# Two of the seven products of each second product taken in seven products of quarters, with attention in a new order between them

## The chip, the cores and the metric

The kernel runs on one core of one Trainium2 chip. Times are device microseconds of that core, from the first to the last instruction and a little around it; the profile's span is some 2 us shorter than the measured time (752.6 of 754.33 us in the profiled run before). A kernel is run several times, interleaved with runs of the kernel before on the same chip (e1 to e4 on one chip, e5 to e12 on another). A kernel counts as faster or slower only from 2% on.

Five engines work side by side: TensorE (PE in the profile; PEld is its weight load), VectorE (DVE), ScalarE (ACT), GpSimd (POOL) and SyncE (SP), in whose queue the transfers that the profile's page lists are issued. In a stretch of 81.61 us of the kernel before, TensorE was busy for 81.61 us, VectorE for 43.77 and ScalarE for 25.99. PSUM is the memory that the matmuls of this code write to; the code uses it in banks, and in the traces TensorE waits until a bank that it writes again has been read out: 0.32 us for one in block 1 of the changed kernel, up to 4.7 us in e10.

## The reference, cut to what matters

```python
# attention: B, H, S, Ns, D = 8, 8, 512, 32, 64, per batch b and head
xread = softmax(x @ state.T / 8) @ state        # 512 rows
sread = softmax(state @ x.T / 8) @ x            #  32 rows
x = concat(xread, sread) -> (8 * 544, 512)
# then two matrix products with an activation between
h = x @ w_in                                    # (4352, 512) @ (512, 2048)
g = h / (1 + exp(-1.702 * h))
out = g @ w_out                                 # (4352, 2048) @ (2048, 512)
```

All of it in float32. The second product, `g @ w_out`, of the 512 rows of a batch is what the change is about.

## The kernel before

A batch is a *block*. The 512 rows of block b go through the first product in an up phase (function `up_strassen`) and through the second in `strassen`. Both use seven products where a two by two split would need eight (the scheme of Strassen and Winograd). `strassen` splits `g` (512 x 2048, held transposed) into four quarters A11 to A22 and `w_out` (2048 x 512) into B11 to B22; S1, S2, S4 are sums of the A, T1 to T4 sums of the B, and S3 stands where A21 was. One of its seven products is this loop, of 16 matmuls with 256 columns (nb = 2, HF = 8, HN = 256):

```python
        def product(ps, lhs, rhs, first):
            for r in range(nb):
                for f in range(HF):
                    nc.tensor.matmul(
                        ps[:, r], lhs[f][:, P * r : P * (r + 1)], rhs[:, f],
                        start=(first and r == 0 and f == 0), stop=(f == HF - 1), skip_group_check=True,
                    )
                if todo:
                    for fn, args in todo.pop(0):
                        fn(*args)
```

After each half of a product comes one *slot*: a list of calls that work on the attention of block b + 1 (and, in the first slot, on the rest of block b's up phase). So attention is spread over the second product of the block in front:

```python
        at(0, att_state, b)
        for j in range(NPR):            # four
            at(j, att_xT, b, j)
        at(5, att_scores, b)
        at(5, att_M, b, 0)
        at(5, att_M, b, 1, True)
        ...                             # the softmaxes
        at(8, att_M, b, 2)
        at(8, att_M, b, 3, True)
        ...
        at(11, att_sread, b)
```

`att_state` and `att_xT` transpose on TensorE into a PSUM pool of two buffers and copy out on ScalarE:

```python
    psA = ctx.enter_context(tc.tile_pool(name="psA", bufs=2, space=bass.MemoryType.PSUM))

    def att_state(b):
        ps = att_ps([P, P], f"stT_{b}")                 # a buffer of psA
        nc.tensor.transpose(ps, stn[b].rearrange("p g d -> p (g d)"), ident)
        A[b]["stT"] = apool.tile([P, P], FP32, tag="stT", name=f"stT_{b}", bufs=2)
        nc.scalar.copy(A[b]["stT"], ps)
```

The end of the up phase, run in the first slot, puts two activations on ScalarE, each behind an addition on VectorE:

```python
        def end(u):
            ...
            add(product(u, "y", l22, t4, False), c21, c21)     # TensorE, then VectorE
            gelu(c21, c21)                                      # ScalarE
            add(product(u, "z", m4, b22, False), c12, c12)
            gelu(c12, c12)
```

Block 0's second product is taken without the scheme, and the 256 rows of `sread` of all batches come last, as a smaller stage (`_sr`).

## Time and profile before

| | before |
|---|---|
| time, median (range) | 754.42 us (754.26 to 754.55), 3 runs |
| span of the profiled run | 752.6 us |
| TensorE busy | 738.5 us, 98% |
| VectorE, ScalarE busy | 432.5 us (57%), 233.1 us (31%) |
| period of blocks 2 to 6 | 81.61 us |
| granted TensorE clock | 0.999 |

The period is the distance of the same instruction in two neighbouring blocks. It is the sharpest number here: it repeats to 0.01 us from block to block.

### The profile page before, as it was taken

What the parts mean: (1) busy time and instruction counts of PE and PEld (TensorE: products, weight loads), DVE (VectorE), ACT (ScalarE), POOL (GpSimd) and SP (SyncE); (2) the same over time, 40 slices, a digit from 0 to 9 for tenths busy, and PEclk for the clock granted to TensorE, in tenths of its full rate; (3) what the DMA queues carried; (4) which work ended last, traced back from release to release, by engine and by line L of the source; (5) the groups of instructions that cost most, each with busy time, mean ns of one, the idle gap of its engine ahead of it and who ended that gap; (6) DMA issues with size and microseconds to landing.
All of it is one profiled execution on the core that took longest, in us unless ns stands there. A gap on an engine that the chain in (4) does not pass through costs nothing.

```text
span 752.6 us, 10076 instructions
## 1 busy us (share of the span) xinstructions
PE 738.5 (98%) x4265; PEld 564.6 (75%) x4267; DVE 432.5 (57%) x744; ACT 233.1 (31%) x415; POOL 0.8 (0%) x8
## 2 busy tenths in 40 slices
PE   8989999999999999999999999999999999999997
PEld 3433444467888878887788788887888778888996
DVE  5999799642646383645637264638355563762341
ACT  4676511022324241433134232424143313300210
POOL 0000000000000000000000000000000000000000
PEclk9999999999999999999999999999999999999999
DMA  9811245010030000300030003000030000000000
GB/s 234 332 57 56 93 160 144 0 57 1 28 86 4 1 15 31 72 1 15 29 74 0 1 29 84 6 1 15 29 74 1 15 29 15 0 15 29 15 1 28
DMA packets 48764, 35.24 MB, mean 47 GB/s; under 512 B 36432, under 2 KB 44112, under 8 KB 48720
## 3 DMA queue, kind: packets, MB, share of 16 engines
q1 hardware_dynamic: 48720, 34.61, 16.0%
q8 instruction: 33, 0.54, 0.3%
q14 instruction: 11, 0.09, 0.0%
HBM read 25.69 MB, written 8.91 MB: 46 GB/s over the span
## 4 chain that ended last, share of the span: by engine, by line
PE 96%; SPq 2%; ACT 1%; DMA 1%; issue 0%; DVE 0%; ACTq 0%
PE y L483 19%; PE z L483 13%; PE x L483 13%; PE upy L614 8%; PE h L418 8%; PE o L436 7%; PE upz L614 6%; PE upx L614 6%; PE M L272 4%; PE xT L254 2%; PE upy_sr L614 1%; PE y_sr L483 1%; SPq L131 1%; PE sr L367 1%; PE s L272 1%; PE upz_sr L614 1%
## 5 line engine op out<-in xcount | busy, mean ns | idle before, releaser
L483 PE MATMUL x<-w_out,g 128*128 128x256 f32 x448 | 100.2, 379 | 0.0
L483 PEld LDWEIGHTS x<-w_out,g 128*128 128x128 f32 x448 | 84.3, 190 | 11.2 <-ACT osb L443 0.2
L624 DVE TENSOR_TENSOR g<-upy,g 128x512 f32<-128x512 f32 x72 | 48.1, 689 | 68.4 <-PE upy L614 68.4
L621 ACT ACTIVATE g<-g 128x512 f32<-128x512 f32 (+1 forms) x84 | 49.8, 600 | 100.5 <-DVE g L624 100.5
L347 ACT COPY M<-M 128x512 f32<-128x512 f32 x64 | 33.2, 596 | 95.1 <-PE M L272 95.1
L418 PE MATMUL h<-aT,M 128*128 128x512 f32 x128 | 58.2, 600 | 4.4 <-ACT M L347 4.4
L418 PEld LDWEIGHTS h<-aT,M 128*128 128x128 f32 x128 | 23.6, 190 | 36.7 <-issue 24.4
L483 PE MATMUL z<-sums,later 128*128 128x256 f32 x224 | 51.1, 382 | 0.0
L483 PE MATMUL z<-w_out,g 128*128 128x256 f32 x224 | 50.8, 382 | 0.0
L483 PE MATMUL y<-sums,later 128*128 128x256 f32 x224 | 50.5, 379 | 0.0
L483 PE MATMUL y<-sums,g 128*128 128x256 f32 x224 | 50.5, 379 | 0.0
L483 PE MATMUL y<-w_out,g 128*128 128x256 f32 x224 | 50.1, 382 | 0.0
L483 PEld LDWEIGHTS z<-sums,later 128*128 128x128 f32 x224 | 42.1, 190 | 10.4 <-issue 5.0
L483 PEld LDWEIGHTS y<-w_out,g 128*128 128x128 f32 x224 | 42.1, 190 | 10.4 <-issue 5.0
L614 PE MATMUL upx<-aT,M 128*128 128x256 f32 x192 | 49.3, 379 | 0.0
L614 PE MATMUL upy<-ta,M 128*128 128x256 f32 x192 | 49.3, 379 | 0.0
L483 PEld LDWEIGHTS z<-w_out,g 128*128 128x128 f32 x224 | 41.7, 190 | 6.1
L483 PEld LDWEIGHTS y<-sums,g 128*128 128x128 f32 x224 | 41.7, 191 | 5.1
L483 PEld LDWEIGHTS y<-sums,later 128*128 128x128 f32 x224 | 41.7, 191 | 5.1
L500 DVE TENSOR_TENSOR osb<-z,later 128x512 f32<-128x512 f32 x14 | 9.7, 692 | 58.4 <-PE z L483 58.4
L614 PEld LDWEIGHTS upy<-ta,M 128*128 128x128 f32 x192 | 36.5, 190 | 4.9
L614 PEld LDWEIGHTS upx<-aT,M 128*128 128x128 f32 x192 | 36.5, 190 | 4.9
(147 smaller groups left out, 1028.0 us busy)
## 6 DMA issues: line engine op xcount, KB each, us to landing
later<-in_moe_w_out_dram SPq DMA_DIRECT2D x16, 512.0 KB
out_dram<-osb SPq DMA_DIRECT2D x32, 256.0 KB
xn<-in_x_dram SPq DMA_DIRECT2D x28, 256.0 KB
w_out<-in_moe_w_in_dram SPq DMA_DIRECT2D x12, 512.0 KB
later<-in_moe_w_in_dram SPq DMA_DIRECT2D x4, 512.0 KB
sums<-in_x_dram SPq DMA_DIRECT2D x4, 256.0 KB
stn<-in_state_dram SPq DMA_DIRECT2D x16, 32.0 KB
out_dram<-osb_sr SPq DMA_DIRECT2D x4, 128.0 KB
```

The source lines that it names most:

```text
L131: nc.sync.dma_start(xn[b][:, c], x_v[b, c])
L254: nc.tensor.transpose(ps[:, c], x_heads(b, c, j), ident)
L272: nc.tensor.matmul(ps[g][st], A[b]["stT"][rows, st], rhs(rows, j), start=True, stop=True)
L347: nc.scalar.copy(m[:, g], ps[g])
L367: nc.tensor.matmul(ps[st, g], a["eT"][:, g, c, st], xn[b][:, c, NG * j + g], start=(c == 0), stop=(c == SCH - 1),)
L418: nc.tensor.matmul(hps, lhs[i], rhs[i], start=(i == 0), stop=(i == n - 1))
L436: nc.tensor.matmul(ops, G[key, f // 2][:, f % 2, P * r : P * (r + 1)], w_out[:, f], start=(f == 0), stop=(f == NF - 1))
L483: nc.tensor.matmul(ps[:, r], lhs[f][:, P * r : P * (r + 1)], rhs[:, f], start=(first and r == 0 and f == 0), stop=(f == HF - 1), skip_grou ...
L500: nc.vector.tensor_tensor(out=o, in0=ps, in1=with_, op=ALU.add)
L614: nc.tensor.matmul(ps[:, k], lhs[i][:, o : o + P], rhs[i], start=(first and k == 0 and i == 0), stop=(i == n - 1), skip_group_check=True,)
L621: nc.scalar.activation(out=dst, in_=src, func=AF.Gelu_apprx_sigmoid)
L624: nc.vector.tensor_tensor(out=dst, in0=ps, in1=x, op=ALU.add)
```

## The change

The intent: in blocks 2 to 7, two of the seven products, S2 T2 and S3 T3, are themselves taken by the scheme of seven, on quarters of their operands. A product of 16 matmuls with 256 columns becomes 28 matmuls with 128 columns, half the width, so 14 instead of 16 by columns. The price is additions on VectorE. Results are no longer accumulated in PSUM over two products but added by VectorE, some buffers are halved in number to make room, and attention is put into other slots. The core of the diff, with cuts:

```diff
-    opool = ctx.enter_context(tc.tile_pool(name="opool", bufs=2))
+    opool = ctx.enter_context(tc.tile_pool(name="opool", bufs=1))
...
+    def strassen_low(left, right, bank, R, at):
+        b11, t3, b21, b22, t1, t2, t4 = right
+        a11, a12, a21, a22, s1, s2, s4 = left
+        p, u2, u3 = (pu[:, i] for i in range(3))
+        o = [v[:, :P] for v in bank]
+        def product(ps, lhs, rhs):
+            for f in range(QF):                      # four
+                nc.tensor.matmul(ps, lhs[f], rhs[:, f], start=(f == 0), stop=(f == QF - 1))
+        ...
+        product(o[0], a11, b11)
+        nc.scalar.copy(p, o[0])
+        at(1)                                        # a hook: a piece of attention on VectorE
+        product(o[1], s2, t2)
+        add(u2, o[1], p)
+        at(2)
+        product(o[2], a12, b21)
+        add(c11, o[2], p)
+        at(3)
+        product(o[0], a21, t3)
+        add(u3, o[0], u2)
+        at(4)
+        product(o[1], s1, t1)
+        add(c22, o[1], u3)
+        add(c12, o[1], u2)
+        at(5)
+        product(o[2], a22, t4)
+        add(c21, o[2], u3)
+        at(6)
+        product(o[0], s4, b22)
+        add(c12, o[0], c12)
...
+    def strassen_two(key, dst, hooks):               # order of its products, with the names of their hooks
+        # P1 = A11 B11, P2 = A12 B21, P5 = S1 T1, P6 = S2 T2 (low), P4 = A22 T4, P7 = S3 T3 (low), P3 = S4 B22
...
+    def hooks_next(b):
+        at("P1a", att_state, b)
+        at("P1a", att_xT, b, 0)
+        at("P1a", att_xT, b, 1)
+        at("P1b", att_xT, b, 2)
+        at("P1b", att_xT, b, 3)
+        at("P2a", att_scores, b)
+        at("P2a", att_M, b, 0)
+        at("P2a", att_M, b, 1, True)
...
+        at("P4a", att_sread, b)
+        at("P4a", att_M, b, 3, True)
+        at("P4a", att_M, b, 2)
...
+        hooks["P1a"] = [(rest, ())] + hooks.get("P1a", [])   # rest: end of the up phase
```

"P1a" is the slot after the first half of P1, and so on. I call the two products taken in quarters the *low* products.

## The prediction

> **What bounds the kernel now.** I read the page first (busy time of each engine), then stretches of one attention block each, then the groups by shape, then the timeline in the order of the code.
>
> ```profile
> span 752.6 us, 10076 instructions
> PE 738.5 (98%) x4265; PEld 564.6 (75%) x4267; DVE 432.5 (57%) x744; ACT 233.1 (31%) x415; POOL 0.8 (0%) x8
> ```
>
> TensorE leads. Blocks 2 to 6 are alike: the chain that ended last finds the same first product at 240.06, 321.67, 403.28, 484.89 and 566.50, one period of 81.61. The stretch of block 3:
>
> ```profile
> 321.67:403.28 81.61, 81.61 (x507) 68.45 (x507) 43.77 (x72) 25.99 (x46) 0.00 (x0) 1.00 0.12 27
> ```
>
> PE fills all of it, VectorE 54% and ScalarE 32%. So a TensorE microsecond removed counts in full, and so does every wait that the change puts in front of TensorE; VectorE has 37.8 us of room.
>
> The price of a matmul comes from start-to-start distances, since 379 ns in the groups is one record's duration and records overlap. Rows of the timeline, N=256 and N=128 (the `_sr` stage at the end already runs float32 matmuls with 128 columns and one weight load each):
>
> ```profile
> 389.30 1.03 PE L614 MATMUL upx<-aT,M 128*128 128x256 f32 x4
> 390.17 1.03 PE L614 MATMUL upy<-ta,M 128*128 128x256 f32 x4
> ...
> 702.49 1.06 PE L614 MATMUL upx_sr<-srT,w_in 128*128 128x128 f32 x8
> 703.38 1.06 PE L614 MATMUL upy_sr<-ta_sr,ws 128*128 128x128 f32 x8
> ```
>
> A program matmul in float32 leaves two records: the loop over two groups of two blocks with 8 pieces is 16 matmuls, and the chain shows x32 for it, 6.91 us. Hence N=256 costs 0.863/2 = 0.432 us a matmul and N=128 0.893/4 = 0.223 us: half the columns cost 52%, although weight loads double per column.
>
> [...] The trace has 112 ns a record[...]. I use the 112.
> [...] (below: the copy of `stT` starts after two gelus although its transpose was long done). This carries my main loss.
> [...] The trace has 0.69 us for 512 and 0.42 for 256[...].
>
> **The change, part by part.**
>
> *Products.* In blocks 2 to 7, two of seven products (16 matmuls, N=256, 6.91 us) become seven of four matmuls, N=128: 28 x 0.2234 = 6.25 us. Saving 0.65 each, 12 of them: **-7.8 us**. That is the whole possible gain, 1.0%. The saving is small because 28 halves are 14 whole ones, and the 112 against 108 ns takes back a third of the two saved.
>
> *VectorE work.* Rows used:
>
> ```profile
> L461 DVE TENSOR_TENSOR later<-later,g 128x512 f32<-128x512 f32 x28 | 19.4, 692 | 1.0
> L537 DVE TENSOR_TENSOR ta<-aT 128x256 f32<-128x256 f32 x12 | 5.0, 417 | 0.0
> ```
>
> A 128x128 add is extrapolated to 0.29 us. Per block the change adds 2x7 such adds (4.1), four 512-wide left sums (2.8), eight 256-wide ones (3.4), two whole additions (k2+k1, k3+k2: 1.4) and, net, one result addition that ScalarE copied before (0.7), while the two removed k2/k3 adds (1.4) are about balanced by t01 and the halved softmax steps (0.7+0.7). Sum 12.4: 43.8 becomes 56 of 81 us, 69%. Not a bound on average. In order of the code, with P2's start at 0: score transposes 4.7 to 6.0, maxima to 7.5, the halved softmax to 10.2, the first result, S4 and the last left sum to 13.0, state normalisation to 14.6. The first low product starts at 16.6. Inside it each step of PE is 4 x 0.223 = 0.89 us, and VectorE has one add (0.29) plus a hook (0.66), 0.95; three PSUM banks rotate, so a bank is wanted again only two steps (1.8 us) after its product ended. Worked through step by step, bank 1 is read at 18.9 and wanted at 20.1, bank 0 20.8 against 21.9. No wait. The sums for the second low product end at 27.5, its start is 33.5; VectorE is clear at 32.6. I find no PE wait there, with about 1 us of margin.
>
> *Attention order.* The first slot (after half of P1) now holds the transposes of the state, of xT 0 **and** of xT 1. They share a PSUM pool of two buffers, so xT 1 waits for ScalarE's copy of `stT`. Before, xT 1 came 3.5 us later. Same place in block 3:
>
> ```profile
> 326.47 0.14 PEld L245 LDWEIGHTS stT<-ident,stn 128*128 128x128 f32 x1
> ...
> 326.75 0.63 ACT L621 ACTIVATE g<-g 128x512 f32<-128x512 f32 x1 [2.96 <-DVE g L624]
> 326.79 0.60 PE L254 MATMUL xT<-ident,xn 128*128 128x128 f32 x4
> ...
> 327.23 3.62 PE L483 MATMUL x<-w_out,g 128*128 128x256 f32 x16
> ...
> 327.61 0.63 ACT L621 ACTIVATE g<-g 128x512 f32<-128x512 f32 x1 [0.23 <-DVE g L624]
> 328.15 0.25 ACT L247 COPY stT<-stT 128x128 f32<-128x128 f32 x1
> ```
>
> The two gelus of the last up products come first in ScalarE's queue, and each waits for a VectorE add. The copy ends at 328.40; TensorE would be ready at 327.23. With 0.1 us to the weight load and 0.2 more to the first matmul, it resumes at 328.7: a wait of about 1.45 us. Blocks 2 to 6 have it (block 7 has no attention after it): **+7.2 us**, which eats the gain.
>
> The pieces of `sr`, M3 and M2 now stand in one slot. A change between full-array and small-tile matmuls costs some 0.1 us on each side (the 16 records after an M run take 3.56 instead of 3.45) and 0.16 within the M run. One such visit less in six blocks, partly kept between two tile shapes: estimate 0.2 each, **-1.2 us**. M2's second bank waits for the `sr` copy, which ends 0.5 us after, while M3 takes 0.86: hidden.
>
> *Buffers.* One `osb` buffer instead of two. At the end of block 0 ScalarE's four copies now each wait for a store (the third copy started at 158.69, 2.2 us after the first ended): the last ends near 164.8 instead of 160.1, the gelu behind it 4.6 us later, S2 near 167.0; the product that wants it starts at 167.8. Hidden. In the last stage results come 3.45 us apart and a store takes some 3: at most **+0.2 us** at the tail. The 6 extra sums in block 1 (4.1 us) fall into VectorE's idle time (6 and 7.7 us waits before its products).
>
> Sum: 754.4 - 7.8 + 7.2 - 1.2 + 0.2 = 752.8.
>
> **Rivals.**
> *The full gain*: the wait at xT 1 isn't there (or is mostly covered), giving 754.4 - 7.8 - 1.2 = 745.5. For it: the author moved these on purpose. Against: pool of two, program order[...]. I give it 12%.
> *VectorE sets the pace in the low products*: 0.95 against 0.89 us a step and a serial queue; if it enters late by 3 us, each low product waits 2 to 3 us, 12 x 2 = +24 us, 777. Against: it is clear 1 to 2 us before both, by measured durations. A slip in part, 0.3 us each, gives +4 (757). I give the large one 5%.
> *Weight loads bound at 128 columns*: the load rows read 190 ns each; unhidden that would be 56 x 0.19 = 10.6 us a product, +45 in all. The `_sr` stage refutes it: same loads, 112 ns apart. The left operand there is contiguous as here; I give it 2%.
>
> **Range and chances.** All small terms pull within 1%: the lower end is the full gain with little left over, the upper end the wait plus 0.4 us per low product. Being 2% faster (below 739.3) would need twice the saving that the matmuls can give: 0.01. 2% slower (above 769.5) needs 17 us of new waits beyond the one found: 0.06.
>
> **What would show it.** (1) The products of quarters: records of N=128 0.112 us apart, 6.25 us per low product; if 0.19, the third rival. (2) TensorE idle about 1.4 us at xT's second set in five blocks, released by ScalarE's `stT` copy; if absent, the first rival. (3) Idle of TensorE at the low products released by VectorE: should be under 0.3 us each; more means the second. (4) VectorE near 56 us a block. (5) Periods of blocks 2 to 6 near 81.4 us, block 7 1.3 shorter than before. The prediction fails if a wait that I did not find, most likely on a bank or through VectorE's queue, recurs in each block.

What the trace has: 112 ns a record, the order on ScalarE in which the copy of `stT` starts at 328.15, after the gelus of 326.75 and 327.61, and 0.69 and 0.42 us for an addition of 512 and 256 columns. The sum reads 754.4 - 7.8 + 7.2 - 1.2 + 0.2 = 752.8, from 0.2234 and 0.432 us a matmul in the trace and from estimates by its rows.

## More of the kernel before

The prediction shows the lines and how they are read. One more, VectorE's line in the page's forty slices of the span (a digit is the busy share in tenths), will be compared later:

```profile
DVE  5999799642646383645637264638355563762341
```

From the ninth slice on the digits fall and rise with each block, and many are 2 to 6: VectorE has room.

## The result

The changed kernel takes 753.31 us in the median of 4 runs (752.25 to 754.42), beside 754.48 us (754.26 to 755.7) before in the same rounds. The ratio is 0.9981, with a 95% interval of 0.996 to 1.0002: the same. I had said 752.8.

| | before | after |
|---|---|---|
| span | 752.6 | 750.4 |
| TensorE busy | 738.5 | 731.6 |
| VectorE busy | 432.5 | 501.7 |
| period of blocks 2 to 6 | 81.61 | 81.37 |
| first product of block 1 starts | 160.17 | 159.92 |
| last addition of the last stage starts | 747.41 | 745.52 |

The page of the changed kernel, its first lines and VectorE's line of the slices:

```profile
span 750.4 us, 10915 instructions
...
PE 731.6 (98%) x4555; PEld 567.4 (76%) x4555; DVE 501.7 (67%) x947; ACT 232.1 (31%) x421; POOL 0.8 (0%) x8
...
DVE  5999799615846775567747666677656774768340
```

TensorE has 6.9 us less to do, VectorE 69 us more, and most valleys of its line are filled to 5 to 7. A stretch of one period in block 4 (columns: the stretch, its length, then busy time of PE, PEld, DVE, ACT and POOL, granted clock, share and rate of the transfers):

```profile
402.53:483.90 81.37, 80.31 (x556) 68.93 (x555) 54.33 (x105) 25.87 (x47) 0.00 (x0) 1.00 0.12 28
```

Before, TensorE's busy time equalled the stretch. Now 1.06 us of the 81.37 are idle. The timeline of the changed kernel has the low product as the count said, 8 records of 128 columns every 0.89 us:

```profile
430.88 1.05 PE L597 MATMUL o<-sums,later 128*128 128x128 f32 x8
431.77 1.06 PE L597 MATMUL low<-low,g 128*128 128x128 f32 x8
...
437.13 1.04 PE L399 MATMUL eT<-ident,e 128*128 128x128 f32 x8
```

From 430.88 to 437.13 are 6.25 us, against 6.91 for a whole product. And the idle time is where the prediction put it. The timeline of the same kernel at the start of block 4's second product (start, length, engine, line; in brackets the idle time of the engine before it and what ended it):

```profile
407.61 0.63 ACT L897 ACTIVATE g<-g 128x512 f32<-128x512 f32 x1 [2.96 <-DVE g L900]
407.66 0.60 PE L261 MATMUL xT<-ident,xn 128*128 128x128 f32 x4
...
408.48 0.63 ACT L897 ACTIVATE g<-g 128x512 f32<-128x512 f32 x1 [0.23 <-DVE g L900]
409.01 0.25 ACT L254 COPY stT<-stT 128x128 f32<-128x128 f32 x1
...
409.31 0.42 PEld L261 LDWEIGHTS xT<-ident,xn 128*128 128x128 f32 x4 [1.29 <-ACT stT L254]
409.31 0.66 PE L261 MATMUL xT<-ident,xn 128*128 128x128 f32 x4 [1.05 <-ACT stT L254]
```

The second set of transposes of `xT` starts 0.05 us after ScalarE's copy of `stT` ended, and that copy stands behind two gelus. Over the whole kernel, in the list of waits (us in total, times, longest):

```profile
PEld xT L261 <- ACT stT L254: 6.5, 5, 1.3
PE xT L261 <- ACT stT L254: 5.3, 5, 1.1
```

Five waits, one in each of blocks 2 to 6. The kernel before has no such line.

**Where the 2.2 us of span come from**, by starts in the two traces: 0.25 before block 1 (the traces are that far apart already near 42 us, before the change acts), 0.02 in block 1, 5 x 0.24 = 1.20 in blocks 2 to 6, 1.29 from the first product of block 7 to that of the last stage (73.29 became 72.00), together 2.76; then 0.57 given back in the last stage. In block 7, which has no attention to carry, the gain is just the two low products, 2 x 0.65.

**A difference that belongs to no kernel.** The times of most kernels here, before included, fall on two levels some 1.7 us apart (after: 752.25 and 752.46, 754.15 and 754.42); of e3, e4 and e7 only one level was seen. It arises before block 1. Near 40 us TensorE waits 2.12 us in every trace. The 16 matmuls after this wait, first in the profiled run before, then in that of e3 below, whose code is the same up to there:

```profile
42.17 7.13 PE L418 MATMUL h<-aT,M 128*128 128x512 f32 x16 [2.12 <-ACT M L347]
```

```profile
42.03 8.83 PE L418 MATMUL h<-aT,M 128*128 128x512 f32 x16 [2.12 <-ACT M L347]
```

In e3 the granted clock was 0.71 from 42 to 44 us and 0.50 from 44 to 46, and these matmuls took 1.7 us longer. The fourteen traces split the same way: in six (before, after, e5, e9, e11, e12) the clock stayed at 1.00 and block 1's first product starts at 159.8 to 160.3; in the other eight the clock fell to half after the same wait, the 16 matmuls took 8.6 to 8.8 us, and block 1 starts at 161.4 to 162.1. So I compare periods and distances within a trace rather than spans.

### The profile page after: what moved, and what is told of

The parts are those of the page before. It is cut to its first block, busy times and chain, and to the rows that moved or that the text cites. A ratio compares the mean times of both kernels' runs of the same rounds, so it can differ in the third digit from the quotient of the medians.

```text
span 750.4 us, 10915 instructions
## 1 busy us (share of the span) xinstructions
PE 731.6 (98%) x4555; PEld 567.4 (76%) x4555; DVE 501.7 (67%) x947; ACT 232.1 (31%) x421; POOL 0.8 (0%) x8
## 4 chain that ended last, share of the span: by engine, by line
PE 94%; SPq 2%; ACT 2%; DMA 1%; DVE 1%; issue 0%; DVEq 0%; ACTq 0%
PE o L645 28%; PE o L890 16%; PE o L522 9%; PE h L461 8%; PE o L479 7%; PE low L597 6%; PE upx L890 6%; PE o L597 4%; PE M L279 4%; PE xT L261 1%; SPq L138 1%; PE sr L410 1%; PE o L279 1%; PE upx_sr L890 1%; DMA out_dram<-osb_sr 1%; PE warm L122 1%
## 5 line engine op out<-in xcount | busy, mean ns | idle before, releaser
L900 DVE TENSOR_TENSOR g<-o,g 128x512 f32<-128x512 f32 (+1 forms) x140 | 88.1, 651 | 87.3 <-PE o L890 86.3
L645 PE MATMUL o<-w_out,g 128*128 128x256 f32 x576 | 130.0, 380 | 0.0
L645 PEld LDWEIGHTS o<-w_out,g 128*128 128x128 f32 x576 | 107.4, 190 | 18.1 <-issue 4.2
L890 PE MATMUL o<-ta,M 128*128 128x256 f32 x192 | 49.3, 379 | 0.0
L890 PE MATMUL o<-ta,ms 128*128 128x256 f32 x192 | 48.4, 380 | 0.0
L645 PE MATMUL o<-sums,g 128*128 128x256 f32 x192 | 43.8, 382 | 0.0
L522 PE MATMUL o<-w_out,g 128*128 128x256 f32 x192 | 42.9, 380 | 0.0
L645 PE MATMUL o<-sums,later 128*128 128x256 f32 x192 | 42.4, 379 | 0.0
L522 PEld LDWEIGHTS o<-w_out,g 128*128 128x128 f32 x192 | 36.1, 190 | 6.0 <-issue 1.3
L890 PEld LDWEIGHTS o<-ta,ms 128*128 128x128 f32 x192 | 36.4, 190 | 5.2 <-DVE osb L541 0.3
L890 PEld LDWEIGHTS o<-ta,M 128*128 128x128 f32 x192 | 36.5, 190 | 5.0
L645 PEld LDWEIGHTS o<-sums,later 128*128 128x128 f32 x192 | 36.5, 190 | 5.0
```

The costliest lines, as they stand in the source:

```text
L522: nc.tensor.matmul(ps[:, r], lhs[f][:, P * r : P * (r + 1)], rhs[:, f], start=(first and r == 0 and f == 0), stop=(f == HF - 1), skip_grou ...
L645: nc.tensor.matmul(ps[:, r], lhs[f][:, P * r : P * (r + 1)], rhs[:, f], start=(r == 0 and f == 0), stop=(f == HF - 1), skip_group_check=True,)
L890: nc.tensor.matmul(ps[:, k], lhs[i][:, o : o + P], rhs[i], start=(first and k == 0 and i == 0), stop=(i == n - 1), skip_group_check=True,)
L900: nc.vector.tensor_tensor(out=dst, in0=ps, in1=x, op=ALU.add)
```

## The experiments

The theory to test: the two low products save 0.65 us each, as counted; the wait for the `stT` copy, made by the order of attention together with two buffers and the order on ScalarE (the copy starts at 409.01, behind the gelu of 408.48), takes nearly all of it back; `sread` beside M3 and M2 gives 0.2; VectorE costs nothing yet. Rivals: the wait is only a symptom and moves elsewhere when removed; the low products save less than counted; VectorE already paces them. Each is read mainly from its period, since it repeats to 0.01 us.

### e1: the state's transpose in the other PSUM pool

```diff
-        ps = att_ps([P, P], f"stT_{b}")
+        ps = psH.tile([P, P], FP32, tag="h", name=f"stT_{b}") if spare else att_ps([P, P], f"stT_{b}")
...
-        at("P1a", att_state, b)
+        at("P1a", att_state, b, True)
```

> The changed kernel with the state's transpose in the other PSUM pool (psH), so that xT 1 no longer needs the buffer that ScalarE has to copy out. Theory (the gain of the quarters is eaten by that wait): the five waits of TensorE on ScalarE's stT copy, 1.3 us each in the trace of the changed kernel, go; period of blocks 2 to 6 falls from 81.37 to about 80.05, time from 753.3 to about 746.8 (ratio to before 0.990). Rival (the wait only moves: xT 2, the scores or a low product then wait for the same ScalarE queue): period stays at 81.3 to 81.4 and the time near 753.

Measured: 747.62 us in the median of 4 runs, ratio 0.9904 (0.9888 to 0.9919). Period 80.10. The wait lines of TensorE on `stT` are gone, and none has come in their place. The wait cost 1.27 us a block, 6.4 in all, and it was real time, not a symptom.

### e2: the state first, buffers unchanged

```diff
-        hooks["P1a"] = [(rest, ())] + hooks.get("P1a", [])
+        own = hooks.get("P1a", [])
+        hooks["P1a"] = own[:1] + [(rest, ())] + own[1:]
```

> The changed kernel with both buffers as they are, only the state's transpose and copy issued ahead of the last up products, so that the copy stands in front of the two gelus in ScalarE's queue. Theory (the wait is the queue's order, not the number of buffers alone): same gain as with the other pool, period about 80.05, time about 746.8. Rival (two buffers are too few whatever the order): a wait of TensorE on an xT or stT copy stays, period above 81.

Measured: 747.94 us, ratio 0.9907 (0.989 to 0.9924). Period 80.10. Its timeline:

```profile
405.30 0.27 PE L252 MATMUL stT<-ident,stn 128*128 128x128 f32 x1
...
405.61 0.27 ACT L254 COPY stT<-stT 128x128 f32<-128x128 f32 x1 [1.48 <-PE stT L252]
...
407.14 1.04 PE L261 MATMUL xT<-ident,xn 128*128 128x128 f32 x8
...
408.01 3.62 PE L645 MATMUL o<-w_out,g 128*128 128x256 f32 x16
```

The copy ends at 405.88, while TensorE is still busy with the last up products, and the eight transposes of xT 0 and 1 run as one group at 407.14. So two buffers are enough if the copy that frees one is ahead of the gelus: it is the order in ScalarE's queue together with the number of buffers, and either remedy alone removes the wait (period 80.10 in e1 and in e2).

### e3: only the early transposes, in the kernel before

```diff
-            at(j, att_xT, b, j)
+            at(j // 2, att_xT, b, j)
```

> The kernel before, with xT 0 and 1 in the first slot and xT 2 and 3 in the second, as the change has them; nothing else. Theory: the same wait of about 1.3 us appears in blocks 2 to 6 (block 1 has no up products in front, there about 0.3): period 81.61 becomes 82.9, time 754.4 becomes about 761 (ratio 1.009). Rival (the wait belongs to something else in the change): period stays 81.6.

Measured: 762.79 us, ratio 1.0107 (1.0092 to 1.0122). Period 82.88, 1.27 more than before. Its waits:

```profile
PEld xT L254 <- ACT stT L247: 6.6, 6, 1.3
PE xT L254 <- ACT stT L247: 5.3, 5, 1.1
```

This part of the change by itself makes the wait, in full. The span grew by 8.0 us (760.6 from 752.6) rather than 6.7. Of that, 6.4 are the five periods and 1.6 arose before block 1 (its first product starts at 161.72 instead of 160.17), where the code is the same: the run-to-run difference told above.

### e4: whole products in the new order

The two calls of `strassen_low` become the old loop into one bank, and the sums for the quarters go:

```diff
-        strassen_low(
-            (z11, z12, z21, z22, blocks(q1), blocks(q2), blocks(q4)), (b11, t3, b21, b22, *low2),
-            low_banks(), k2, lambda i: hook(f"P6.{i}"),
-        )
-        tt(k2, k2, k1)
+        product(bank(1), [S2[:, f, :half] for f in range(HF)], T2, "P6")
+        for i in range(1, 8):
+            hook(f"P6.{i}")
+        tt(k2, bank(1), k1)
...                                  # the same for S3 T3; no sums q, v, no low_third
```

> The changed kernel with S2 T2 and S3 T3 taken whole again (16 matmuls of 256 columns) and the sums for their quarters left out; the new order of attention stays. Theory: each block gets 2 x 0.65 longer, period 81.37 becomes 82.67, block 7 likewise: six blocks, +7.8 us, about 761. Rival (quarters save less than the count says, through waits on VectorE or weight loads in the low products): the period gets longer by less than 1.0, and the time stays under 759.

Measured: 761.81 us, ratio 1.0095 (1.0078 to 1.0112). Period 82.68, that is 1.31 more than with quarters, or 0.655 a product against 0.65 counted. Quarters give all that the count promises; no part of it is lost to waits or weight loads. It also shows the change without its point: the new order alone makes a block 1.07 us longer than before (82.68 against 81.61).

### e5: two result buffers again

```diff
-    opool = ctx.enter_context(tc.tile_pool(name="opool", bufs=1))
+    opool = ctx.enter_context(tc.tile_pool(name="opool", bufs=2))
```

> The changed kernel with two osb buffers again. Theory (in the last stage two results wait about 0.4 and 0.9 us for the store of the one before; the copies at the end of block 0 are hidden): the two waits of VectorE on the DMA of osb_sr, 3.4 us each by the profile because TensorE's work falls into them, go; the last addition ends some 0.9 us earlier after the start of the last stage's first product (27.3 becomes 26.4 us), the span 0.9 shorter, time about 752.4. Rival (the copies at the end of block 0 cost too): more than 2 us. Rival (nothing): no difference of that distance.

Measured: 752.25 us in the median of 5 runs, ratio to before 0.9958 (0.9945 to 0.9971); the changed kernel in its own rounds had 0.9981 (0.996 to 1.0002), and the intervals overlap. The traces decide. The changed kernel's list of waits has a line that e5's lacks:

```profile
DVE osb_sr L541 <- DMA out_dram<-osb_sr: 6.9, 2, 3.5
```

The last two additions of the changed kernel:

```profile
741.67 0.42 DVE L541 TENSOR_TENSOR osb_sr<-o,g 128x256 f32<-128x256 f32 x1 [3.46 <-DMA out_dram<-osb_sr]
745.52 0.42 DVE L541 TENSOR_TENSOR osb_sr<-o,g 128x256 f32<-128x256 f32 x1 [3.42 <-DMA out_dram<-osb_sr]
```

From the `stT` copy of block 6 (571.75 and 571.60) to the start of the last addition (745.52 and 744.48) it is 173.77 us with one buffer and 172.88 with two: 0.89. The first of the three expectations holds. A store takes 3.46 us from the end of the addition to the freed buffer (738.21 to 741.67), and the addition of 0.42 comes before it: with one buffer a result can pass every 3.88 us, while TensorE has one ready every 3.45. So each of the last two results is late, the second by more. The copies at the end of block 0 are indeed hidden: block 1's first product starts at 159.76 with two buffers and 159.92 with one.

### e6 and e7: more work for VectorE in the low products

```diff
+        hook = at
+        def at(i):
+            hook(i)
+            nc.vector.tensor_tensor(out=waste[:, :128], in0=waste[:, :128], in1=waste[:, :128], op=ALU.add)
```

(e7: 512 columns instead of 128.)

> The changed kernel with one more, useless VectorE addition of 128 columns (0.29 us) in each of the seven steps of a low product, 12 x 7 = 84 in all. Theory (VectorE has about 1 us to spare there): no wait of TensorE on VectorE, period stays within 0.1 of 81.37. Rival (VectorE already sets the pace of the low products): each low product gets up to 2 us longer, period 83 to 85, time 765 to 775.

> As e6 with 512 columns (0.69 us) in each step. Now a step of VectorE takes 1.6 us against 0.89 of TensorE. By hand: in the first low product bank 0 is read at about 6.3 us after its start and wanted at 5.4, so a wait near 0.5 to 1.5 us; the second starts with VectorE still busy. I expect 1.5 to 5 us more per block, period 83 to 86, time 763 to 785, with TensorE seen waiting for VectorE in the low products. If the period stays near 81.4, the margin is larger than I worked out.

Measured: e6 753.63 us, ratio 0.9971 (0.9956 to 0.9987), period 81.37. e7 754.53 us, ratio 0.9984 (0.9971 to 0.9998), period 81.37 as well. For e6 the theory holds. For e7 my own expectation failed: seven more additions of 512 columns in each low product left the period where it was. Its timeline, VectorE's part and then TensorE's part:

```profile
434.91 0.29 DVE L602 TENSOR_TENSOR pu<-low,pu 128x128 f32<-128x128 f32 x1 [3.26 <-PE low L599]
435.12 0.67 DVE L366 TENSOR_REDUCE sm<-e 128x16 f32<-128x512 f32 x1
435.71 0.68 DVE L609 TENSOR_TENSOR waste<-waste 128x512 f32<-128x512 f32 x1
436.31 0.28 DVE L602 TENSOR_TENSOR later<-low,pu 128x128 f32<-128x128 f32 x1
...
437.53 0.28 DVE L602 TENSOR_TENSOR pu<-o,pu 128x128 f32<-128x128 f32 x1
```

```profile
438.21 1.06 PE L599 MATMUL o<-sums,g 128*128 128x128 f32 x8
```

The low product starts at 432.86. Its bank 0 is wanted again at 438.21, 5.35 us later, as I had said (5.4). But VectorE has read it at 437.81, 4.95 us after the start, not 6.3. I had added durations. Neighbouring VectorE instructions overlap: the 512-wide one of 0.68 us is followed 0.60 later, the 128-wide one of 0.29 only 0.21 later. And the hook between the two additions is the short one (the inverse of 32 columns). So the margin in the low products was larger than I thought: 7 x 0.60 = 4.2 us more VectorE work in each fits, with 0.4 us left at the tightest bank.

### e10: where VectorE does set the pace

Twice the useless addition of 512 columns in each step (a loop of two around e7's line).

> The changed kernel with two useless additions of 512 columns in each step of a low product (e7, with one, left the period at 81.37, against what I had expected: its trace has bank 0 read at 437.8, 0.4 us before the product that reuses it). With two, that read comes 1.2 us later (two of them lie in front of it after VectorE's last idle time), so the last product of the first low one waits about 1 us; VectorE then enters the second low product some 3 us late and TensorE waits there for bank 1 by 2 to 3 us. Theory: period 84 to 86, waits of TensorE on VectorE at the low products in the trace. Rival: it still stays at 81.4, then something other than the banks decouples the two.

Measured: 799.42 us in one run, state unknown; the periods are 88.8 to 89.1. The waits of TensorE on VectorE are there:

```profile
PEld low L599 <- DVE pu L602: 15.6, 6, 4.9
...
PE low L599 <- DVE pu L602: 14.5, 6, 4.7
```

So the rival "VectorE paces the low products" is a real limit, which lies between 4.2 and 8.4 us of added work per low product; the changed kernel is far from it. The period grew more than I expected. The second low product of block 4 shows why, by two groups of its matmuls and by stretches of 2 us (columns as above; the number before the last two is the granted clock):

```profile
472.17 1.44 PE L599 MATMUL low<-low,later 128*128 128x128 f32 x8 [1.95 <-DVE pu L602]
474.30 2.08 PE L599 MATMUL low<-low,g 128*128 128x128 f32 x8 [0.68 <-DVE later L602]
```

```profile
470.00:472.00 2.00, 0.22 (x2) 0.03 (x1) 1.97 (x4) 0.00 (x0) 0.00 (x0) 1.00 0.00 0
472.00:474.00 2.00, 1.44 (x8) 1.15 (x8) 1.97 (x5) 0.00 (x0) 0.00 (x0) 0.72 0.00 0
474.00:476.00 2.00, 1.71 (x8) 1.71 (x8) 1.97 (x5) 0.00 (x0) 0.00 (x0) 0.50 0.00 0
```

TensorE was idle 1.95 us at 470, about what I expected; then its granted clock fell to half, until shortly before 480, and the matmuls there took twice as long (2.08 us for a group of 1.06). The same wait of 1.95 us stands in each of blocks 2 to 6, and the half clock follows it each time. In blocks 3 to 6 the first records after it already ran longer (1.26 to 1.57 us), so the shorter wait behind them isn't what began it; the wait of 0.79 us in each first low product left the clock at 1.00. So it was after the waits of 1.05 us in the changed kernel, and after one of 1.51 us near 50 us in its trace (1.50 in that before). The wait of 1.95 us cost more than itself: this low product took 11.80 us (466.49 to 478.29) instead of 6.25, and only 2.63 of the difference are the two waits.

### e8: M3 and M2 away from sread

```diff
-        at("P4a", att_M, b, 3, True)
-        at("P4a", att_M, b, 2)
+        at("P4b", att_M, b, 3, True)
+        at("P4b", att_M, b, 2)
```

> The changed kernel with M3 and M2 moved out of the slot of sread, to half a product later. Theory (one visit less to small tiles saves 0.2 us a block): period of blocks 2 to 6 grows from 81.37 to 81.5 to 81.7. Rival (adjacency saves nothing): period stays at 81.37 within 0.03.

Measured: 755.1 us, ratio 0.9987 (0.9971 to 1.0002). Period 81.57: one visit more to small tiles costs 0.20 us. The theory holds, with exactly the estimate. The trace shows where: the half product between `sread` and M3 takes 3.65 us (444.93 to 448.58) against 3.45 for one between full-array matmuls, 0.1 on each side. The run of M3 and M2 takes 1.87 us in both orders, so what a visit costs within it isn't saved by the neighbour.

### e9: both repairs

The edits of e2 and e5 together.

> The changed kernel with both repairs: the state's transpose ahead of the last up products, and two osb buffers. Theory: the two gains add, 5 x 1.27 (the period measured there, 80.10 instead of 81.37) and 0.9 at the end: 7.3 us under the changed kernel, ratio to before about 0.989 to 0.990, period 80.1. Rival (one hides the other): no more than either alone, ratio 0.991 or above.

Measured: 746.41 us in the median of 4 runs (745.57 to 747.97), ratio 0.9884 (0.9868 to 0.99). Period 80.10. Its list of waits has no wait of VectorE on the store of `osb_sr` any more, and the last results start 3.40 and 3.45 us apart (731.81, 735.21, 738.66). The span is 743.5 against 750.4 for the changed kernel, 6.9 less where 6.4 + 0.9 = 7.3 were to be had; the rest lies before the change acts, since block 1's first product starts at 160.29 in this trace and at 159.92 in that of the changed kernel. The gains add.

### e11 and e12: a third product in quarters

e7 had shown room on VectorE. So e11 takes A22 T4 in quarters as well, on top of e2's repair, at the end of the block, with its left sums in rooms that are free by then:

```diff
-        product(bank(2), A_of(1, 1), T4, "P4")
+        product(bank(3), A_of(0, 1), B22, "P4")        # the product P3, moved forward
+        ...                                             # left sums of A22 into q1, q2, q4
...
-        product(bank(3), A_of(0, 1), B22, "P3")
+        strassen_low(
+            (xl(0, 0), xl(1, 0), xl(0, 1), xl(1, 1), blocks(w1), blocks(w2), blocks(w4)), (b11, t3, b21, b22, *low4),
+            low_banks(), o10, lambda i: hook({2: "P7", 4: "P3a"}.get(i, "")), 1,
+        )
```

> A version on top of the state-first repair: a third product, A22 T4, taken in quarters too, at the end of the block, with its left sums in rooms that are free by then, the results of the last stage in four rooms of their own (no store waited for). By the count of matmuls another 0.65 us a block: period 80.10 becomes 79.45, block 7 likewise, so 3.9 us less than the kernel with both repairs, ratio to before about 0.984 to 0.985. VectorE gets 5.5 us more a block, about 60 of 79. Rival (VectorE's queue at the end of the block, where the quarters' additions meet those of the next up products, makes TensorE wait): period 80 or more, no gain over the two repairs.

Measured: 748.66 us, ratio 0.991 (0.9895 to 0.9925). Period 80.09: the rival, no gain over e2 and 2 us slower than e9. Its timeline, TensorE at the start of the third low product:

```profile
449.70 1.06 PE L599 MATMUL o<-w_out,later 128*128 128x128 f32 x8
451.14 1.16 PE L599 MATMUL o<-sums,g 128*128 128x128 f32 x8 [0.38 <-DVE later L602]
```

The undisturbed distance is 0.89 us, here it is 1.44. Two low products in a row share their first bank: the last product of one and the first of the next write it, with an addition between them that nobody overlaps. In the last block, moreover, long sums for the last stage stand in VectorE's queue ahead of additions that free a bank (a wait of 1.3 us there).

e12 mends both, by another first bank for the third low product and another order of those sums (which stand in the last block only, so the period tests the bank alone):

```diff
-            low_banks(), o10, lambda i: hook({2: "P7", 4: "P3a"}.get(i, "")), 1,
+            low_banks(2), o10, lambda i: hook({2: "P7", 4: "P3a", 5: "Pe5", 6: "Pe6"}.get(i, "")), 1,
...
-            hooks = {"P3a": steps[9:] + [(low_third, (T2,)), (low_third, (T3,))]}
+            hooks = {"P3a": [(low_third, (T2,)), (low_third, (T3,))], "P4a": steps[8:10], "P4b": steps[10:]}
```

> e11 gained nothing: its trace has period 80.09, with TensorE waiting at the start of the third low product for VectorE's last addition out of the bank that the second one used too (0.55 us a block against the undisturbed distance of the products), and 2.1 us more in the last block, where the sums for the last stage stand in front of the additions. Here the third low product begins in another PSUM bank, and in the last block the four short sums stand where two long ones did, those two come after the last bank that TensorE needs. Theory (the third product's saving was eaten by the bank and by VectorE's order): period 79.5 (80.09 less 0.55), the last block no longer than in e9; 3 to 4 us less than e9, ratio to before 0.983 to 0.985. Rival (VectorE's queue is simply full there): another wait takes the place, period 80.0.

Measured: 743.09 us in the median of 6 runs (741.92 to 743.77), ratio 0.9834 (0.9821 to 0.9846). Period 79.45. A stretch in block 4 (79.40 us of it):

```profile
403.60:483.00 79.40, 79.40 (x580) 69.08 (x579) 58.84 (x121) 26.21 (x48) 0.00 (x0) 1.00 0.12 28
```

TensorE is busy throughout again, VectorE 74%. The period is 80.10 less one saving of 0.65. This version beats both kernels: the quarters were worth their count all along, and each of the three stalls in their way (the copy of `stT`, the shared first bank, the long sums in the last block) was one dependence, a few lines to remove.

## Why the prediction was right

**The size of the gain: right.** "28 x 0.2234 = 6.25 us", a saving of 0.65 a product, -7.8 in all. Measured: 6.25 in the timeline, 0.655 from e4. The price of 128 columns came from the last stage of the kernel before, which runs such matmuls already; the rival of weight loads at 190 ns fell with it, records 0.112 us apart. Two sums of the working are wrong, without harm to the 6.25: 28 x (0.2234 - 0.216) = 0.21 us is a quarter, not a third, of the two matmuls saved (0.86); and the rival of the full gain comes to 745.4, not 745.5.

**The wait at xT 1: right in place, cause and number of blocks, 0.18 us too large.** I had said 1.45 us in blocks 2 to 6. It is 1.27 (e1, e3). The mis-sized term is the restart: I had put 0.1 us to the weight load and 0.2 more to the first matmul after the copy's end, an estimate, and the first transposes start 0.05 after it, load and matmul together. That is 5 x 0.18 = 0.9 us of the sum. That the queue's order makes it, not only the buffers, is shown by e2.

**Attention's small tiles: right,** 0.2 a block (e8). In block 1, for which I had counted it too, the trace shows 0.02 instead. The visit is saved there as well: from the first product to the first up product of block 2 it is 57.24 us instead of 57.43. But the 0.19 is lost right after. The up phase took its banks from a rotating pool of four before; now each of its products has a fixed one, and the second waits for the one that block 1's last addition still reads:

```profile
217.94 1.59 PEld L890 LDWEIGHTS o<-ta,ms 128*128 128x128 f32 x8 [0.32 <-DVE osb L541]
```

That is a wait on a bank that I did not find; blocks 2 to 6 do not have it.

**VectorE: no wait, as said, and the margin larger.** In the changed kernel bank 1 is read at 433.23 and wanted at 434.45 (I had said 18.9 against 20.1, the same 1.2), and the period's busy time is 54.3 us where I had summed 56; durations overlap, so sums of them are too high. e6 and e7 bear the verdict out, e10 shows where it ends.

**The single result buffer: too small.** I had said at most 0.2 us at the tail; e5 measures 0.89. The failing step is "a store takes some 3" (the trace before has SyncE waiting 2.8 us for the last one): it takes 3.46, and with the addition of 0.42 before it one buffer passes a result every 3.88 us where one comes every 3.45, so the lateness of one passes on to the next. The span shows only 0.57 of it, since from the last addition's start to the end were 5.2 us before and 4.9 after, which I can't attribute.

**The sum.** Predicted -1.6 us by the terms, 752.8; the profiled span fell by 2.2, the medians of the same rounds by 1.2, to 753.31. The errors of 0.9 too much for the wait, 0.7 too little for the tail and 0.2 too much gain in block 1 nearly cancel, so the closeness of the total is partly luck; the terms are right to 0.2 us a block.

Undecided stays why the same wait of 2.12 us near 40 us is followed by a cut of the clock in some runs and not in others.

## What to carry to other kernels

When one engine is busy all the time, count what an arithmetic saving is worth in its own spacing (half the columns cost 52% here), and then go through every new place where that engine's next instruction needs a buffer: the saving of 1.3 us a block was undone by one copy of 0.25 us that stood behind two gelus in ScalarE's queue. Look for what frees a buffer and in which queue it stands; moving it ahead cost nothing here (e2), and another buffer did as well (e1). A helper used twice in a row can meet itself in its own first bank, and an engine that looks full by summed durations may have room, since these overlapped here (VectorE's instructions of 0.68 us were followed 0.60 us later in e7); only the distance of starts tells.
